# Down projection of one layer: two array tiles of 128x64 side by side in place of whole-array matmuls

## The chip, the cores and the metric

One core of one Trainium2 chip. The metric is device time in microseconds for one launch. Runs in the fast state (granted TensorE clock 0.994 to 1.000) may be compared with each other. Medians are quoted. Ratios are the mean time of one kernel's fast runs over that of the other's of the same rounds, so not quite the ratio of the medians.

## The reference

Four sublayers on a stream of 2048 rows by 1024 columns, in bf16: linear attention, gated block, linear attention, gated block, each on a layer norm of the stream and added to it. The change is in the gated block:

```python
def _B_ref(x, w_gate, w_up, w_down):      # x 2048x1024, gate and up 1024x3584, down 3584x1024
    g = jnp.einsum("bsd,df->bsf", x, w_gate)
    u = jnp.einsum("bsd,df->bsf", x, w_up)
    h = g * u
    return jnp.einsum("bsf,fd->bsd", h, w_down)
```

## The kernel before

The gated block works on groups of 512 rows. For each group, gate and up are multiplied first (448 matmuls), with the product kept transposed as `hT`. Then the group's four output tiles of 128 rows follow, `d_unit`: for each of the 28 steps `f` of the contraction, two matmuls of 512 columns accumulate into two PSUM banks.

```python
    def both(ps, lhsT, rhs, start, stop):
        for n in range(2):
            nc.tensor.matmul(out=ps[:, n, :], lhsT=lhsT, rhs=rhs[:, n * NB:(n + 1) * NB], start=start, stop=stop)
    # ... cut ...
    def d_unit(t, last):
        def run():
            ps = mm_tile()                     # 128 x 2 x 512 float32, one of three buffers
            tl = t % TPG
            for f in range(KF):                # KF = 28
                both(ps, hT[:, f, tl * P:(tl + 1) * P], wd[f], f == 0, f == KF - 1)
            add_store(t, 0, D, flat(ps), last) # VectorE adds it to the stream
        return run
```

Elsewhere the kernel already uses array tiles. The small products `kv` (128x32 tiles, four side by side, 32 columns) and `quarter` (32x32 tiles, 16 at once, 512 columns) give a matmul a `tile_position`.

## Time and profile before

| | before |
|---|---|
| median (2 runs) | 1626.3 us |
| TensorE (PE) busy | 1620.1 of 1624.7 us |
| share of PE in the chain of waits | 100% |
| down projection, second layer | 4 stretches of 48.35 us |
| one matmul of 512 columns, start to start | 48.35 / 224 = 0.2159 us |

The page of before: busy time and share of the span, with the number of instructions, by engine (PE the matmuls, PEld the weight loads).

```profile
PE 1620.1 (100%) x8129; PEld 735.3 (45%) x8129; DVE 609.4 (38%) x895; ACT 287.3 (18%) x389; POOL 54.5 (3%) x136
```

The chain of waits of before, in order of time, in the middle of the second layer: start in us, duration in us, what ran. L199 is the down projection, L523 gate and up.

```profile
331.47 48.35 PE ps L199 x224
379.82 96.69 PE ps L523 x448
476.51 48.35 PE ps L199 x224
```

The stretches join without a gap, and every engine but PE waits (busy for 45% of the span or less, PE for 100%): **whatever the change adds to or takes from the PE's stream of matmuls, it adds to or takes from the time.** A slot is 0.2159 us. The 379 ns that the profile gives for one matmul is its latency, and neighbours, which start 215 or 216 ns apart, overlap in it; it must not be multiplied by a count.

The groups of weight loads of before (the down projection's are in this group; busy us, mean ns):

```profile
L199 PEld LDWEIGHTS <-R 128*128 128x128 bf16 x1736 | 169.9, 98 | 204.8
```

A load is 98 ns on record and there is one for each slot of 216 ns. By the single records it starts about 2 ns after the preceding matmul: it is hidden under the streaming.

### The profile page before, as it was taken

The page shows a single profiled execution, that of the slowest core. Times are in us where ns is not written, and L with a number is a line of the kernel's source. Part 1 is how long each engine was busy: PE and PEld are TensorE (multiplying, and loading weights), DVE is VectorE, ACT ScalarE, POOL GpSimd, SP SyncE. Part 2 cuts the span into 40 slices and gives each one's busy share as a digit, 9 for nine tenths or more (in the row PEclk, how much of TensorE's full clock was granted, in tenths as well). Part 3 has the DMA queues.
Part 4 walks back from the last instruction along what each step waited for, and adds up shares of the span by engine and source line. Part 5 has one row for each costly group of instructions (what it writes and reads, how often), then busy time and mean ns, then how long its engine had stood idle before and what let it go on. Part 6 is the DMA issues. An engine that isn't in the chain of part 4 may idle for free.

```text
span 1624.7 us, 18711 instructions
## 1 busy us (share of the span) xinstructions
PE 1620.1 (100%) x8129; PEld 735.3 (45%) x8129; DVE 609.4 (38%) x895; ACT 287.3 (18%) x389; POOL 54.5 (3%) x136
## 2 busy tenths in 40 slices
PE   9999999999999999999999999999999999999999
PEld 4444444444444444444444444444444444444444
DVE  6789853212311321243245798432123113211111
ACT  5533201101110110011045222011011101101110
POOL 2100000000000000010000000000000000000000
PEclk9999999999999999999999999999999999999999
DMA  7325856511550452142420358555235406521400
GB/s 236 57 71 105 234 162 175 162 52 53 165 171 0 139 160 90 52 156 63 91 55 1 78 104 243 151 170 162 71 96 173 134 20 172 165 66 65 156 0 26
DMA packets 235937, 182.87 MB, mean 113 GB/s; under 512 B 101456, under 2 KB 216656, under 8 KB 235856
## 3 DMA queue, kind: packets, MB, share of 16 engines
q1 hardware_dynamic: 235856, 181.69, 39.2%
q8 instruction: 63, 1.03, 0.3%
q14 instruction: 18, 0.15, 0.0%
HBM read 153.09 MB, written 4.19 MB: 97 GB/s over the span
## 4 chain that ended last, share of the span: by engine, by line
PE 100%; ACT 0%; DVE 0%; issue 0%
PE ps L523 48%; PE ps L199 44%; PE ps L291 7%; PE ps L550 1%; PE kv L310 0%; PE ps L169 0%; PE pm L334 0%; PE pt L406 0%; ACT GL L294 0%; DVE xT L409 0%; DVE X L531 0%; DVE xT L164 0%; PE ps L334 0%
## 5 line engine op out<-in xcount | busy, mean ns | idle before, releaser
L523 PE MATMUL ps<-xT,R 128*128 128x512 bf16 x2432 | 528.5, 379 | 0.0
L523 PEld LDWEIGHTS <-R 128*128 128x128 bf16 x2432 | 238.0, 98 | 286.9
L527 DVE TENSOR_TENSOR R<-gs,ps 128x512 bf16<-128x512 f32 x224 | 153.8, 687 | 533.6 <-ACT gs L526 533.6
L526 ACT COPY gs<-ps 128x512 f32<-128x512 f32 x224 | 131.0, 585 | 1040.4 <-PE ps L523 1040.4
L199 PEld LDWEIGHTS <-R 128*128 128x128 bf16 x1736 | 169.9, 98 | 204.8
L523 PE MATMUL ps<-xT,W 128*128 128x512 bf16 x1152 | 251.6, 379 | 0.0
L199 PEld LDWEIGHTS <-xT 128*128 128x128 bf16 x1536 | 148.7, 98 | 178.9 <-issue 1.8
L199 PE MATMUL ps<-W,xT 128*128 128x512 bf16 x1024 | 225.3, 380 | 0.3 <-DVE xT L409 0.3
L523 PEld LDWEIGHTS <-W 128*128 128x128 bf16 x1152 | 112.7, 98 | 136.0
L199 PE MATMUL ps<-W,R 128*128 128x512 bf16 x744 | 170.7, 379 | 0.0
L531 DVE TENSOR_TENSOR X<-X,ps 128x1024 bf16<-128x1024 bf16 (+3 forms) x34 | 39.4, 1158 | 335.8 <-PE ps L199 326.1
L291 PE MATMUL ps<-R,R 128*128 128x512 bf16 x512 | 112.8, 379 | 0.0
L199 PE MATMUL ps<-PQ,R 128*128 128x512 bf16 x496 | 112.1, 379 | 0.0
L199 PE MATMUL ps<-R,xT 128*128 128x512 bf16 x512 | 110.8, 379 | 0.0
L204 ACT ACTIVATE e<-ps 128x1024 bf16<-128x1024 f32 x56 | 57.3, 1024 | 145.5 <-PE ps L199 145.5
L178 DVE BATCH_NORM_STATS2 st<-X 128x6 f32<-128x512 bf16 x128 | 81.9, 681 | 1.9 <-DMA X<-in_A_x_dram 1.8
L291 PEld LDWEIGHTS <-R 128*128 128x128 bf16 x512 | 49.8, 98 | 59.6
L182 POOL TENSOR_SCALAR ve<-mv 128x1 f32<-128x1 f32 x64 | 16.7, 260 | 1330.4 <-DVE mv L180 1330.4
L199 PE MATMUL ps<-GL,R 128*128 128x512 bf16 x248 | 58.6, 379 | 0.0
L199 PE MATMUL ps<-xT,R 128*128 128x512 bf16 x248 | 58.6, 379 | 0.0
L377 DVE TENSOR_TENSOR X<-X,ps 128x1024 bf16<-128x1024 bf16 x32 | 38.6, 1212 | 26.6 <-PE ps L199 26.6
L189 DVE TENSOR_SCALAR R<-X,mv,rstd 128x1024 bf16<-128x1024 bf16 x64 | 33.9, 542 | 23.9 <-POOL rstd L184 23.9
(64 smaller groups left out, 474.5 us busy)
## 6 DMA issues: line engine op xcount, KB each, us to landing
R<-in_B_w_gate_dram SPq DMA_DIRECT2D x38, 1024.0 KB, 5.4
R<-in_B_w_up_dram SPq DMA_DIRECT2D x38, 1024.0 KB, 7.4
W<-in_B_w_gate_dram SPq DMA_DIRECT2D x18, 1024.0 KB, 5.6
W<-in_B_w_up_dram SPq DMA_DIRECT2D x18, 1024.0 KB, 7.4
W<-in_A_wqkv_dram SPq DMA_DIRECT2D x10, 1024.0 KB, 5.9
W<-in_B_w_down_dram SPq DMA_DIRECT2D x6, 1024.0 KB, 11.5
PQ<-in_B_w_down_dram SPq DMA_DIRECT2D x4, 1024.0 KB, 7.9
X<-in_A_x_dram SPq DMA_DIRECT2D x15, 256.0 KB, 5.4
```

The lines of the kernel that those rows point to most:

```text
L178: nc.vector.bn_stats(out=st[:, c, :], in_=X[:, t, c * NB:(c + 1) * NB])
L182: nc.gpsimd.tensor_scalar(out=ve[:], in0=mv[:, 1:2], scalar1=1e-5, scalar2=None, op0=ALU.add)
L189: nc.vector.tensor_scalar(out=dst, in0=X[:, t, :], scalar1=mv[:, 0:1], scalar2=rstd[:], op0=ALU.subtract, op1=ALU.mult)
L199: nc.tensor.matmul(out=ps[:, n, :], lhsT=lhsT, rhs=rhs[:, n * NB:(n + 1) * NB], start=start, stop=stop)
L204: nc.scalar.activation(out=e[:], in_=flat(ps), func=ACT.Exp, **sc)
L291: nc.tensor.matmul(out=ps[:, n, :], lhsT=XN[:, t, m * P:(m + 1) * P], rhs=PK[:, t, n * NB:(n + 1) * NB], start=(t == 0), stop=(t == NT - 1))
L377: nc.vector.tensor_tensor(out=X[:, t, :], in0=X[:, t, :], in1=flat(ps), op=ALU.add)
L523: nc.tensor.matmul(out=ps[:, n, :], lhsT=w[:, k, j * P:(j + 1) * P], rhs=xT[g % 2][:, k, :], start=(k == 0), stop=(k == KD - 1))
L526: nc.scalar.copy(out=gs[:], in_=ps[:, 0, :])
L527: nc.vector.tensor_tensor(out=hT[:, f, :], in0=gs[:], in1=ps[:, 1, :], op=ALU.mult)
L531: nc.vector.tensor_tensor(out=X[:, t, a:b], in0=X[:, t, a:b], in1=ps, op=ALU.add)
L550: nc.tensor.matmul(out=ps[:, 0, 0:b - a], lhsT=hT[:, f, tl * P:(tl + 1) * P], rhs=wd[f][:, a:b], start=(f == 0), stop=(f == KF - 1))
```

## The change

The 128x128 weight tile of each matmul is cut in two halves of 64 columns, which go to the left and the right half of the array. Each half streams the same 512 moving columns and writes its own 64 partitions of the same PSUM bank. Only the second layer's down projection is touched; the fourth layer keeps `both`. The intent, it seems, was to have two smaller matmuls running at once.

```diff
+    def halves(ps, lhsT, rhs, start, stop):
+        for n in range(2):
+            for i in (0, 64):
+                nc.tensor.matmul(out=ps[i:i + 64, n, :], lhsT=lhsT[:, i:i + 64], rhs=rhs[:, n * NB:(n + 1) * NB],
+                                 start=start, stop=stop, tile_position=(0, i))
@@ d_unit
             for f in range(KF):
-                both(ps, hT[:, f, tl * P:(tl + 1) * P], wd[f], f == 0, f == KF - 1)
+                if last:
+                    both(ps, hT[:, f, tl * P:(tl + 1) * P], wd[f], f == 0, f == KF - 1)
+                else:
+                    halves(ps, hT[:, f, tl * P:(tl + 1) * P], wd[f], f == 0, f == KF - 1)
```

## The prediction

> **What bounds the kernel now.** TensorE. The page gives PE 1620.1 of 1624.7 us busy; the chain of waits puts 100% of the span on PE; the granted clock is 1.00. The chain in order of time shows the second layer's down projection as four stretches of 48.35 us (from 331.5, 476.5, 621.6 and 766.6), each 224 whole-array matmuls: 215.9 ns from start to start, 193.4 us in all. The 379 ns given for one matmul is latency, not its share of the array. Its weight load (98 ns) starts about 2 ns after the preceding matmul and is wholly hidden.
>
> **What the change does.** In these stretches each of the 896 matmuls 128x128x512 becomes two of 128x64x512, on the left and right half of the array: 896 matmuls and 896 weight loads more. No arithmetic, data, semaphore edge or DMA is added or removed; the other engines' order is the same. The fourth layer keeps whole-array matmuls.
>
> **Costs.**
> 1. If the halves ran one after the other, 896 x 215.9 = 193 us would be added. I think they don't. The kernel already packs tiles: 16 matmuls of 32x32x512, four side by side in every row strip, start about 3 ns apart, and the next whole-array matmul starts 0.36 us after the first of them; in turn they would need 3.4 us. So a pair should take one slot of 215.9 ns. There is no gain either: both halves stream all 512 columns.
> 2. Weight loads. [...] My estimate is 100 to 120 ns on record for 64 columns (128x32 took 93). It matters only if not hidden. In the KV products (128x32 tiles, four side by side) a tile's next weight load is issued 1.7 ns after its matmul and its next matmul follows 25 ns after the last, so loads overlap the tile's own matmul. Under 215 ns of streaming they should vanish. [...]
> 3. Issue. Four instructions per 216 ns in place of two. In two KV units back to back, [...] a load and a matmul still came every 8.3 ns: far from binding.
> 4. Mode switches. [...] into the KV tiles 309 ns passed between matmul starts in place of 216, and about 100 ns extra on leaving the 32x32 tiles. Eight switches at 95 ns: 0.8 us.
> 5. A fixed cost for a second matmul in a slot, 0 to 3 ns: 0 to 3 us.
>
> All of this is on PE, so on the critical path; nothing is removed.
>
> **Prediction.** 1626.3 + 0.8 + about 0.7 = 1627.8 us; 8 in 10 within 1626.2 to 1635. Faster by over 2%: 0.01; within 2%: 0.89; slower by over 2%: 0.10.
>
> **What would show it.** The four stretches last 48.5 to 49.5 us each; matmuls of a pair start about 3 ns apart, pairs 216 ns apart; twice the matmul and weight-load records there (some may be missing); PEld busy up by 50 to 100 us with no PE idle; later stages shifted by a constant, otherwise unchanged; about 0.1 us lost at each of eight mode switches.
>
> **What would make it wrong.** Weight loads not hidden when two tiles share all 128 rows [...]; two tiles obstructing each other by reading the same moving columns at nearly the same time, where the existing packed matmuls read different ones; tiles serialised at 128 rows (pairs 430 ns apart, about 1820 us). A lower time would refute the account of slots.

## The result, and the profile after

| | before | after |
|---|---|---|
| median (2 runs each) | 1626.3 us | 1627.31 us |
| ratio, 95% interval | | 1.0006 (0.9986 to 1.0026) |
| span of the profiled run | 1624.7 us | 1625.5 us |

The same time, by the 2% rule. The interval of the whole runs even includes no change at all; the difference of about 1 us is read from the traces, which resolve it.

The page of after:

```profile
PE 1621.0 (100%) x9025; PEld 748.4 (46%) x9025; DVE 609.8 (38%) x895; ACT 287.5 (18%) x389; POOL 54.5 (3%) x136
```

There are 896 matmuls and 896 loads more, and 0.9 us more of busy PE. The chain of waits of after in the same part (L205 is `halves`, L530 gate and up):

```profile
331.43 48.47 PE ps L205 x448
379.89 96.80 PE ps L530 x448
476.69 48.47 PE ps L205 x448
```

A stretch of down projection now holds 448 matmuls in place of 224 and lasts 48.47 us in place of 48.35. The gate and up stretch behind it, which did not change, lasts 96.80 in place of 96.69. So about 0.12 us is lost on going into the tiles and 0.11 us on coming out; four times both is about 0.92 us. (By the start times of the single records it is 0.91 us, 0.113 us a switch; the expectations below were written with 0.93 and 0.116.) In between nothing is lost. (In the second gated block, where both kernels use the whole array, the stretches are 48.35 and 96.69 us in both traces, 0.85 us later in after, whose first stretch of tiles had begun 0.04 us earlier.)

The weight loads of the tiles, in the groups of after:

```profile
L205 PEld LDWEIGHTS <-R 128*64 128x64 bf16 x1792 | 101.2, 110 | 92.7 <-issue 1.7
```

A load of 64 columns takes 110 ns on record, longer than that of 128 columns (98 ns), yet it is not seen in the time. The start times of single records in after, in ns from the first of a stretch, show the pattern:

```
242 matmul | 243 load | 245 matmul | 247 load | 458 matmul | 459 load | 461 matmul | 463 load | 673 matmul ...
```

Two matmuls start 3 ns apart, and the next two 216 ns later. Each load starts 2 ns after a matmul and has some 200 ns to finish.

### The profile page after: what moved, and what is told of

It is laid out like the page before. It is cut to its first block, busy times and chain, and to the rows that moved or that the text cites. A ratio compares the mean times of both kernels' runs of the same rounds, so it can differ in the third digit from the quotient of the medians.

```text
span 1625.5 us, 20503 instructions
## 1 busy us (share of the span) xinstructions
PE 1621.0 (100%) x9025; PEld 748.4 (46%) x9025; DVE 609.8 (38%) x895; ACT 287.5 (18%) x389; POOL 54.5 (3%) x136
## 4 chain that ended last, share of the span: by engine, by line
PE 100%; ACT 0%; DVE 0%; issue 0%
PE ps L530 48%; PE ps L199 32%; PE ps L205 12%; PE ps L298 7%; PE ps L560 1%; PE kv L317 0%; PE ps L169 0%; PE pm L341 0%; PE pt L413 0%; ACT GL L301 0%; DVE xT L416 0%; DVE X L538 0%; DVE xT L164 0%; PE ps L341 0%
## 5 line engine op out<-in xcount | busy, mean ns | idle before, releaser
L530 PE MATMUL ps<-xT,R 128*128 128x512 bf16 x2432 | 528.5, 379 | 0.0
L530 PEld LDWEIGHTS <-R 128*128 128x128 bf16 x2432 | 237.7, 98 | 287.4 <-issue 0.8
L530 PE MATMUL ps<-xT,W 128*128 128x512 bf16 x1152 | 251.6, 379 | 0.0
L530 PEld LDWEIGHTS <-W 128*128 128x128 bf16 x1152 | 112.7, 98 | 136.0 <-issue 0.4
L205 PEld LDWEIGHTS <-R 128*64 128x64 bf16 x1792 | 101.2, 110 | 92.7 <-issue 1.7
L199 PEld LDWEIGHTS <-R 128*128 128x128 bf16 x840 | 82.2, 98 | 99.1
L205 PE MATMUL ps<-W,R 128*64 128x512 bf16 x768 | 88.2, 379 | 0.0
L199 PE MATMUL ps<-W,R 128*128 128x512 bf16 x360 | 82.6, 379 | 0.0
L298 PEld LDWEIGHTS <-R 128*128 128x128 bf16 x512 | 49.8, 98 | 59.6
L205 PE MATMUL ps<-PQ,R 128*64 128x512 bf16 x512 | 58.0, 379 | 0.0
L199 PE MATMUL ps<-PQ,R 128*128 128x512 bf16 x240 | 54.2, 379 | 0.0
```

The source lines that it names most:

```text
L205: nc.tensor.matmul(out=ps[i:i + 64, n, :], lhsT=lhsT[:, i:i + 64], rhs=rhs[:, n * NB:(n + 1) * NB], start=start, stop=stop, tile_position= ...
L298: nc.tensor.matmul(out=ps[:, n, :], lhsT=XN[:, t, m * P:(m + 1) * P], rhs=PK[:, t, n * NB:(n + 1) * NB], start=(t == 0), stop=(t == NT - 1))
L530: nc.tensor.matmul(out=ps[:, n, :], lhsT=w[:, k, j * P:(j + 1) * P], rhs=xT[g % 2][:, k, :], start=(k == 0), stop=(k == KD - 1))
```

## The experiments

The theory after the result had four parts. (1) A tile is a stream of its own: a matmul holds its tile for its 512 columns, however few array columns it uses, and two tiles run at once, so a pair is one slot. (2) The loads are hidden. (3) The extra 0.9 us is eight mode switches. (4) Matmuls start in program order. Three of the parts held; the fourth fell.

All experiments edit `halves` of the changed kernel, or its call (for long runs also `d_unit` around it), and so touch the second layer's down projection alone, except the one that says otherwise.

### Is a pair two full streams, or two half-priced matmuls in turn?

Both readings give the same time for the change itself: one slot for a pair. The first two experiments tell them apart.

**Both halves in the left tile** (result wrong, but for the first and last `f`):

```diff
-                nc.tensor.matmul(out=ps[i:i + 64, n, :], ..., tile_position=(0, i))
+                o = i if start or stop else 0
+                nc.tensor.matmul(out=ps[o:o + 64, n, :], ..., tile_position=(0, o))
```

> In the four down stretches of the second layer, every right-half matmul except those of the first and last f goes into the LEFT tile (wrong result on purpose); instructions, shapes and loads are those of the changed kernel. Theory (two tiles are two independent streams; every matmul holds its tile for 512 columns, 215.9 ns, however few array columns it uses): 16 x 26 x 2 = 832 matmuls lose their partner, +832 x 215.9 ns = +179.6 us over the changed kernel, about 1807 us, stretches of 93.4 us. Rival 'half the columns, half the time' (a 128x64 matmul takes half a slot and the two run in turn): no change, 1627 us.

Measured: 1807.33 us, ratio 1.1113 (1.1096 to 1.1129). The stretch in the chain of waits:

```profile
332.15 93.36 PE ps L206 x448
```

The instructions are those of the changed kernel (the same count of matmuls and loads), and only the place in the array differs: 1807.33 - 1627.31 = 180.0 us, against 179.6 us expected. A matmul 64 array columns wide costs a full slot. The tiles' running side by side is what pays for it.

**The left half only** (wrong): the right-half matmuls are left out except at the first and last `f`.

```diff
             for i in (0, 64):
+                if i == 64 and not (start or stop):
+                    continue
```

> The right-half matmuls of all f but the first and last are left out (wrong result on purpose): 832 of 1792 matmuls and their weight loads are gone. Theory of independent streams: the left half alone still needs 215.9 ns a slot, so the time stays at 1627.3 us within 0.6 us. Rival 'half the columns, half the time': 832 x 108 ns less, about 1537 us. Rival 'a small fixed cost of the second matmul in a slot of about 1 ns makes the +1 us': back to about 1626.4 us and stretches of 48.35 us; the theory that the +1 us is mode switches keeps them at 48.47 us.

Measured: 1627.45 us, ratio 1.0006 (0.9991 to 1.0021); the stretches:

```profile
331.48 48.47 PE ps L207 x240
379.94 96.80 PE ps L532 x448
```

With 208 of 448 matmuls gone from the stretch, it lasts as long as with all of them. The right tile is free of charge, and the 0.12 us is not a cost of the pairs. So half of the array's columns gain nothing by working alone, and nothing is lost by adding the other half. A rival for the +180 us of the kernel before falls too, namely that two matmuls in turn in one tile were held up because they write the same PSUM bank: here, and in the runs of 14 to 112 below, one tile's matmuls alternate between two banks and still come 216 ns apart.

The comparison with the reference says little of this sublayer. An estimate from the scales in the reference shows why: its output is about 1e-4 on a stream of about 0.05, below what bf16 keeps of it. Correctness of such a change has to be argued from the indices.

### How much room is there for loads and issue?

**Four tiles of 128x32**: eight instructions in a slot.

```diff
-            for i in (0, 64):
-                nc.tensor.matmul(out=ps[i:i + 64, n, :], lhsT=lhsT[:, i:i + 64], ...
+            for i in (0, 32, 64, 96):
+                nc.tensor.matmul(out=ps[i:i + 32, n, :], lhsT=lhsT[:, i:i + 32], ...
```

> Four tiles of 128x32 in place of two of 128x64: 8 instructions in a slot in place of 4, four weight loads. Theory: still one slot of 215.9 ns, loads and issue hidden, 1627.3 us within 0.8 us, stretches of 48.5 us. Rival 'the weight loads or the issue are just barely hidden with two tiles': stretches of 50 us and more, over 1633 us.

Measured: 1627.45 us, ratio 1.0007 (0.9990 to 1.0023). Still one slot:

```profile
331.48 48.46 PE ps L205 x896
```

**Nearly all matmuls of the kernel in halves.** `both` is replaced by `halves`, and the matmuls of gate, up and G are cut in the same way.

> Nearly every whole-array matmul of 512 columns in the kernel (query, key, G, output projection, gate, up, both down projections but the last row) is split into the two tiles: about 7,300 pairs in place of 896. Theory (no cost in a slot, a cost at each mode switch only; the eight switches around the down projection are gone, others come at the transposes, the 32-wide tiles and the last row, as many as there were within a few): 1626.3 us within 1.0 us. Rival 'about 1 ns a pair': 1634 us. [...]

Measured: 1627.57 us (1627.02 to 1628.35), ratio 1.0007 (0.9994 to 1.0021). The median lies 0.3 us above the range that I gave, so the expectation was missed narrowly. The chain of waits in the middle of the kernel shows where it held:

```profile
332.49 48.35 PE ps L201 x448
380.83 96.69 PE ps L529 x896
477.53 48.35 PE ps L201 x448
```

These are before's durations to 0.01 us, with twice the matmuls, and the 0.12 us at the joints is gone: no switch, no cost. The missed microsecond is at the start. The end of the first long stretch came at 91.65 us in place of 90.81. By the start times of the single records 0.52 us of this was lost where PE waited for weights of the first layer (the profile puts 0.36 us of idle time there, and the chain goes through that DMA). The other 0.30 us was lost in the first 11 us, where whole-array transposes and tile matmuls take turns, in steps of which the largest are about 0.1 us, the size of a mode switch. Whether the wait for weights belongs to the edit or to this one execution is not shown.

**Short streams.** To see the loads at all, they need less to hide under. The same down projection was run with moving operands of 128 and of 64 columns, in whole-array matmuls and in halves; each short matmul has its own load.

```diff
         for n in range(2):
-            for i in (0, 64):
-                nc.tensor.matmul(out=ps[i:i + 64, n, :], lhsT=lhsT[:, i:i + 64], rhs=rhs[:, n * NB:(n + 1) * NB],
-                                 start=start, stop=stop, tile_position=(0, i))
+            for c in range(0, NB, W):                               # W = 128 or 64
+                for i, w in ((0, 64), (64, 64)):                    # whole: ((0, P),), no tile_position
+                    nc.tensor.matmul(out=ps[i:i + w, n, c:c + W], lhsT=lhsT[:, i:i + w],
+                                     rhs=rhs[:, n * NB + c:n * NB + c + W], start=start and c == 0, stop=stop,
+                                     skip_group_check=True, tile_position=(0, i))
```

The theory under test was that the loads of the tiles are only just hidden under 512 columns and show under fewer; the rivals in the expectations of the halves are that they cost no more than those of the whole array. The 56 ns expected of a whole-array matmul of 128 columns are what the transposes of before show (eight of 128 columns, 56 ns from start to start); the 29 ns of 64 columns are an estimate, on a straight line through that and the 215.9 ns of 512 columns.

128 columns, whole array:

> Down projection of the second layer in whole-array matmuls of 128 columns in place of 512, each with its own weight load: 3584 in place of 896. Streaming of 512 columns in 215.9 ns[...]: 128 columns about 56 ns if the load (98 ns on record, most of it latency) is hidden: 3584 x 56 = 201 us, +7 us, 1634 us. If the load occupies more than 56 ns of the array or of its path, the spacing is that instead.

128 columns, halves:

> The same 128-column matmuls as pairs of 128x64 tiles: 7168 matmuls and loads. [...] the spacing of pairs exceeds that of the whole-array kernel once a load of 64 columns[...] times one or two no longer fits in 56 ns; [...] Rival 'the two tiles load side by side and as fast as the whole array': the same time as the whole-array kernel of 128 columns, within 2 us.

64 columns, whole array:

> Whole-array matmuls of 64 columns: 7168. If streaming alone counts, 29 ns each, 208 us, 1641 us. [...]if the spacing is larger than 35 ns the load, the issue or the fetch of instructions sets it.

64 columns, halves:

> Pairs of 128x64 tiles of 64 columns: 14336 matmuls and loads. [...] Rival 'loads of both kinds cost the same': the whole-array kernel's time within 3 us. A confound: if instructions come no faster than 8.3 ns for a load with its matmul (seen in the KV products), a pair needs 17 ns, so issue does not bind here unless it is slower for long stretches.

| | time | ratio (95%) | from start to start, by the single records |
|---|---|---|---|
| 128 columns, whole | 1633.19 us | 1.0042 (1.0027 to 1.0057) | 55.8 ns (50.03 us / 896) |
| 128 columns, halves | 1649.11 us | 1.0142 (1.0127 to 1.0157) | 56 ns a pair |
| 64 columns, whole | 1651.59 us | 1.0152 (1.0137 to 1.0167) | 29 ns |
| 64 columns, halves | 1847.62 us | 1.1351 (1.1332 to 1.1369) | 32 ns a pair |

The whole-array rows fit an estimate from 512 and 128 columns (215.9 and 55.8 ns): 0.417 ns a column and 2.4 ns for each matmul, which for 64 columns makes 29.1 ns.

The times alone would have misled. The last row is 196 us above the one before it, 27 ns for each of the 7168 pairs, as if the loads of the tiles were longer and showed. But the pairs come 32 ns apart, only 3 ns more than whole-array matmuls. The time is elsewhere, as the chain of waits of 64 columns in halves shows at the start of its first stretch:

```profile
331.55 2.96 PE ps L206 x179
334.51 3.50 issue
338.01 3.42 PE ps L206 x128
341.42 0.31 issue
341.74 2.21 PE ps L206 x128
343.95 1.24 issue
```

PE runs 128 matmuls with their 128 loads, then nothing comes for 0.3 us to 3.5 us, then 128 again. "Issue" is time in which PE waited for nothing that the profile shows. Its groups of weight loads (the last number is idle time of the load engine before them) sum it up for the whole array and for halves, at 64 columns:

```profile
L206 PEld LDWEIGHTS <-R 128*128 128x128 bf16 x7168 | 211.7, 99 | 8.3 <-issue 7.4
```

```profile
L206 PEld LDWEIGHTS <-R 128*64 128x64 bf16 x14336 | 242.3, 115 | 176.9 <-issue 176.9
```

Of the 196 us, about 170 us is this idle time; 7168 pairs at 3 ns more make 22 us of the rest. At 128 columns the halves have the same breaks, which account for the 16 us between the first two rows of the table. The loads of the whole array and of the halves, and a piece of the chain of the halves:

```profile
L206 PEld LDWEIGHTS <-R 128*128 128x128 bf16 x3584 | 200.4, 98 | 0.9
```

```profile
L206 PEld LDWEIGHTS <-R 128*64 128x64 bf16 x7168 | 201.7, 110 | 17.1 <-issue 15.3
```

```profile
360.11 3.76 PE ps L206 x128
363.87 0.24 issue
364.11 3.76 PE ps L206 x128
```

This looks like the supply of instructions. The page's instruction queue (packets, MB, share) moved 2.75 MB in 168 packets, about 16 KB each. Its packets grow with the program: 63 in before, 70 in after and 168 here, for 18711, 20503 and 45454 instructions, which is 256 and 255 more instructions for each further packet. And 256 instructions, a block, stand between two breaks.

```profile
q8 instruction: 168, 2.75, 0.6%
```

Two things in the kept traces tie the breaks to that queue. First, the spacing depends little on what is computed: breaks that are one block apart are 3.45 to 4.29 us apart at 64 columns and 3.73 to 4.57 us at 128 columns in halves (median 3.74 and 3.75), although PE needs about 2.1 us for such a block in the one and 3.6 us in the other. Second, each of the 107 breaks (of over 0.15 us) at 64 columns ends 1.20 to 1.61 us after a packet of that queue landed, and each after a different packet; the 32 breaks of the 128-column halves end 1.21 to 1.67 us after one. For example, packets landed at 336.57, 340.22 and 343.78 us, and PE went on at 338.01, 341.74 and 345.19. So between breaks one block apart, an instruction came every 13.5 to 16.8 ns on average (3.45 to 4.29 us over 256), where four in 32 ns would be one every 8 ns. The four tiles at 512 columns need one every 27 ns and show no break. No run here changes the supply alone, and why a block takes this long is not shown.

What the runs show of the loads: a load of 64 columns into a tile is hidden under 128 columns of streaming (56 ns a pair, against 55.8 ns for the whole array), and under 64 columns all but 3 ns at most (32 against 29 ns; that these 3 ns are the load was not tested). The theory that the loads were only just hidden is refuted. And a load's record is a latency, like a matmul's: in whole-array matmuls of 64 columns, loads of 99 ns on record follow each other every 29 ns.

### What is the extra microsecond?

**Whole-array matmuls at even `f`, tiles at odd `f`**: 448 mode switches in place of 8.

```diff
-                if last:
+                if last or f % 2 == 0:
                     both(ps, hT[:, f, tl * P:(tl + 1) * P], wd[f], f == 0, f == KF - 1)
```

> Whole-array matmuls at even f, two tiles at odd f: 28 mode switches for each of 16 output rows, 448 in place of 8, and half as many split pairs. Theory (the +0.93 us of the changed kernel is 8 switches of 0.116 us): +448 x 0.116 = +52 us over before, about 1678 us, stretches of 61 us. Rival 'the +0.93 us is 896 pairs at 1.04 ns each': 448 pairs, +0.5 us, 1626.8 us. Rival 'a switch costs only where the stage changes too (another PSUM buffer, another operand to wait for)': below 1630 us.

Measured: 1677.29 us, ratio 1.0312 (1.0297 to 1.0328): 1677.29 - 1626.32 = 50.97 us, 0.114 us a switch, against 0.116 expected. Four of the pairs' pieces in the chain of waits:

```profile
331.87 0.55 PE ps L205 x4
332.96 0.55 PE ps L205 x4
334.05 0.55 PE ps L205 x4
335.14 0.55 PE ps L205 x4
```

They recur every 1.09 us. Four slots in that period are 0.863 us, which leaves 0.113 us for each of two switches. The rivals (a cost of each pair; a switch that costs only at a change of stage) fall.

### Does program order decide what overlaps?

The change puts the halves in turn: left, right, left, right. If matmuls start strictly in program order, longer runs in one tile must leave the other idle. Three kernels hold the same matmuls in other orders.

**Runs of two** (the loops over `n` and `i` exchanged):

```diff
-        for n in range(2):
-            for i in (0, 64):
+        for i in (0, 64):
+            for n in range(2):
```

> The same matmuls as in the changed kernel, the two loops exchanged: left n=0, left n=1, right n=0, right n=1. Theory (matmuls start in program order; each tile streams by itself): the second left matmul starts 216 ns after the first, the right tile's first one 3 ns after it, so left and right still overlap, shifted by one: a slot of 216 to 219 ns, 1627.3 to 1630.5 us. Rival 'only a pair that starts together runs side by side': left n=0 and right n=1 run alone, 1.5 slots a pair, 896 x 108 ns = +97 us, 1724 us. Rival 'neighbours overlap only if they are two by two in order': 2 slots, 1820 us.

Measured: 1627.15 us, ratio 1.0006 (0.9992 to 1.0020); stretches of 48.47 us. This is the value that two theories share.

**Runs of four** (`f` and `f + 1` in one tile, then in the other):

```diff
+        # ... cut: d_unit calls this at even f ...
+        for i in (0, 64):
+            for g in (f, f + 1):
+                for n in range(2):
+                    nc.tensor.matmul(out=ps[i:i + 64, n, :], lhsT=hT[:, g, tl * P + i:tl * P + i + 64],
+                                     rhs=wd[g][:, n * NB:(n + 1) * NB], start=g == 0, stop=g == KF - 1, tile_position=(0, i))
```

> The same again in runs of four in one tile (n=0, 1 of f and of f+1), then four in the other. Theory of program order: left at 0, 216, 432, 648; right from 651 to 1299; the next left at 1302: four pairs in 1302 ns, 325 ns a pair in place of 216, +896 x 109.6 ns = +98 us, about 1725 us, stretches of 73 us. Rival 'the engine looks ahead in its queue and starts the other tile's matmuls early': 1627.3 us.

Measured: 1627.42 us, ratio 1.0007 (0.9993 to 1.0020).

```profile
331.14 48.49 PE ps L206 x448
379.63 96.80 PE ps L532 x448
```

My theory of program order fell: 98 us were expected and none came. By the single records the first right matmul starts 13 ns after the first left one, though four left ones stand before it. The right tile's matmuls did not wait for the left tile's four that stand before them.

**Runs of 112, 56, 28 and 14**, one length for each of the four stretches, to find out how far this goes:

```diff
+        # ... cut: d_unit, which makes the lists of work ...
+        for i in (0, 64):
+            for ps, f, tl in work:        # 14, 7 or more steps f; for 112, two output tiles at once
+                for n in range(2):
+                    nc.tensor.matmul(out=ps[i:i + 64, n, :], lhsT=hT[:, f, tl * P + i:tl * P + i + 64],
+                                     rhs=wd[f][:, n * NB:(n + 1) * NB], start=f == 0, stop=f == KF - 1, tile_position=(0, i))
```

> How far ahead does the other tile start? The four stretches use runs of 112, 56, 28 and 14 matmuls in one tile (with their weight loads 224, 112, 56 and 28 instructions), then as many in the other; same matmuls, same order within a tile. Theory A: a tile's next matmul may pass those waiting for the other tile within a window of W instructions; the second tile then lags by (run - W/2) slots, and only that lag is lost, once for each stretch, since the first tile meanwhile goes on. [...] With a window of 16: 70.9, 58.8, 52.8, 49.8 us. Rival B, strict program order (2 x (run - 1)/run slots a pair): 96, 95, 93 and 90 us, 1808 us. Rival C, a queue for each tile without bound: 48.5 us in all four, 1627.3 us.

Measured: 1774.08 us, ratio 1.0909 (1.0891 to 1.0927). The stretches, in the chain of waits:

```profile
330.99 94.31 PE ps L206 x448
...
522.10 90.98 PE ps L206 x448
...
709.88 84.31 PE ps L206 x448
...
890.99 70.98 PE ps L206 x448
```

None of the three lists of numbers fits; strict order (96, 95, 93 and 90 us) comes nearest in the first two stretches and fails by 19 us in the last. What fits is a short look-ahead, counted at each change of tile. Take off 0.12 us for the mode switch, divide by the slot of 0.21585 us, and compare with 448 slots, the time with no overlap at all:

| run | changes of tile in the stretch | slots taken | slots overlapped | overlapped for each change |
|---|---|---|---|---|
| 112 | 3 | 436.4 | 11.6 | 3.9 |
| 56 | 7 | 420.9 | 27.1 | 3.9 |
| 28 | 15 | 390.0 | 58.0 | 3.9 |
| 14 | 31 | 328.3 | 119.7 | 3.9 |

At each change the next tile starts about four slots before the last tile has finished, whatever the length of the run. The runs of two and of four, which overlapped wholly, agree with this. A run has such an overlap at each end, so by an estimate from 3.9 runs of up to seven would also overlap wholly; none between 4 and 14 was tried. The step of my theory A that failed is "only that lag is lost, once for each stretch": that holds while the window is at least half a run, and with a window of four the lag is paid again at each change.

The records show the passing itself. In the last stretch the program order begins with 30 matmuls whose moving operand lies in tile PQ (14 left, 14 right, then the first 2 of the next left run), then 12 in W (left), then 2 in PQ (right). The records are in order of start time:

```profile
890.92 5.18 PE L206 MATMUL ps<-PQ,R 128*64 128x512 bf16 x29
895.75 0.38 PE L206 MATMUL ps<-W,R 128*64 128x512 bf16 x1
895.93 0.38 PE L206 MATMUL ps<-PQ,R 128*64 128x512 bf16 x1
895.97 1.89 PE L206 MATMUL ps<-W,R 128*64 128x512 bf16 x8
897.48 0.40 PE L206 MATMUL ps<-PQ,R 128*64 128x512 bf16 x1
897.69 0.38 PE L206 MATMUL ps<-W,R 128*64 128x512 bf16 x1
897.72 0.38 PE L206 MATMUL ps<-PQ,R 128*64 128x512 bf16 x1
```

A W matmul starts at 895.75, before the last of the 30 PQ ones at 895.93, and the right run's two PQ matmuls start after 9 and 10 of the 12 W ones: matmuls of different tiles have exchanged places. At the changes of tile in these records the next tile's first matmul starts 6 or 7 ns after the fourth from last of the run before it. The compiler is not what exchanged them: the instruction stream of TensorE holds the runs as written (4, 8, 16 and 32 runs of 112, 56, 28 and 14 matmuls, and 448 of four). By what mechanism they pass each other is not shown; the runs give only how far, 3.9 slots at each change.

## Why the prediction was right

The prediction was 1627.8 us, with a range of 1626.2 to 1635; measured 1627.31 us.

1. *"So a pair should take one slot of 215.9 ns. There is no gain either."* Right, and shown from both sides: the same pair in one tile costs a second slot (+180.0 us), and the left half without the right one costs no less.
2. *Weight loads vanish under the streaming.* Right. The load's record was estimated at 100 to 120 ns and is 110 ns. Why a load half as wide has the longer record (110 against 98 ns) is not shown. The tiles' loads cost nothing at 512 columns, and at most 3 ns a pair at 64.
3. *Issue is far from binding.* Right at 512 columns: eight instructions in a slot also cost nothing. It has a limit that I did not foresee: the 8.3 ns for a load with its matmul was read from a burst of 16, and held no longer; between the breaks of the long stretches a load with its matmul came every 27 to 34 ns on average (halves at 64 columns, 3.45 to 4.29 us over 128). The change needs one every 108 ns, so the conclusion stood.
4. *Eight switches at 95 ns: 0.8 us.* That each switch costs time was right, and the size a little small: 0.113 us each by the single records, 0.114 us by the 448 switches, 0.91 us in all.
5. *"A fixed cost for a second matmul in a slot, 0 to 3 ns"*, entered with about 0.7 us. It is nil: the stretches with every matmul split last 48.35 us, as before.

Terms 4 and 5 erred in opposite directions by 0.1 and 0.7 us, so that the total is 0.5 us off; that it came so near is in small part luck. One side statement was wrong: "PEld busy up by 50 to 100 us". It rose by 13.1 us. Busy time counts overlapping records once, and the two loads of a pair start 3 ns apart; I had added them as if they came in turn. "Stretches of 48.5 to 49.5 us" was just missed too, at 48.47.

Part (4) of the theory, program order, was not needed for the prediction, since the change alternates the tiles. It would have misled in a change that does not.

No version here beats both kernels, and none was to be expected from tiles: the array streams in every slot already, and splitting it neither shortens a stream nor leaves one out.

## What to carry to other kernels

Count a matmul by the columns that it streams and by the array tile that it holds, not by its area: narrowing the weights to half of the array saves nothing unless another, useful matmul runs in the other half at the same time (a stretch took 48.47 us with 240 matmuls, most of them in the left half alone, and with 448; in one tile, 93.36 us). Array tiles pay where a weight tile is narrower than the array anyway: in `quarter` 16 matmuls of 32x32x512 start about 3 ns apart, and the next whole-array matmul 0.36 us after the first of them, where 16 slots would be 3.4 us by an estimate from 0.2159 us a slot. Cutting a full tile was neutral at 512 columns, and each switch between tiling modes cost about 0.114 us, so keep tiled and untiled work in long blocks. Put matmuls of different tiles in turn, or in short runs: runs of two and four cost nothing here, runs of 14 made a stretch of 48.47 us into one of 70.98. And cutting doubles the instructions: with short moving operands that cost 16 us more at 128 columns and 196 us at 64 (of which about 170 us in breaks that look like the supply of instructions).
